# Turning the second head pair's q and k on TensorE in the prologue, another bank for the first row maximum, and two weight forms three products later

## The chip, the cores and the metric

The kernel runs on one core of one Trainium2 chip. The metric is the time of one execution of the program on the device in microseconds. The engines are TensorE (PE; its weight loads are PEld), VectorE (DVE), ScalarE (ACT), GpSimd (POOL) and SyncE (SP); SP, ACT and POOL also issue DMA transfers.

## The reference

Routed attention over 4 batches, 8 heads, 768 tokens and head size 64, and behind it a feed-forward block over 3072 tokens, 512 model columns and 2048 hidden columns. All inputs are float32.

```
q_n, k_n, c_n = q, k, centroids, each row divided by its norm
q_assign = argmax over the 16 clusters of q_n . c_n        (k_assign likewise)
scores = (q @ k.T) / 8, and -1e9 where q_assign != k_assign
attn   = softmax(scores) along the keys
x      = attn @ v, heads side by side            # 3072 x 512
h      = x @ w_in                                # 512 x 2048
g      = h * erf(softplus(h))
out    = g @ w_out                               # 2048 x 512
```

## The kernel before

**Attention.** Heads go in pairs: 16 pairs of one batch and two heads, each pair with the two heads' 64 dimensions side by side on the 128 partitions. For pair `p` the kernel needs q and k turned, with dimensions on partitions and 768 tokens along the row (`rows[p % 3]`, called `qT` and `kT`). The normal way there: `load` brings q (or k) in pieces of 32 tokens by 32 dimensions, four loads a tensor, 128 bytes at a time, in such an order that one VectorE instruction over 128x768, which turns each 32x32 block (`ve.transpose` in `transposes`), gives `qT`. For pair 1 the load goes into `x_more`, a tile that later holds other things: right behind the turn of pair 1's k, `fetch(PLACES - 1)` loads a block of `w_in` into it. v is loaded with tokens on partitions, two loads a pair, 256 bytes at a time.

A pair then goes through these steps. `similarities` multiplies by the centroids, `choose` finds each token's cluster on VectorE, and `masks` writes cluster rows `qm` and `km` (ScalarE or VectorE copies them from PSUM). `vectors` makes bf16 copies `qv` and `kv`. `maxima_step(p, i, sm)` makes, for one of six tiles of 128 queries and one half of the keys, masked scores in the PSUM tile `sm` by a pass of `kv` with `qv` and a pass of `km` with `qm`, and one VectorE reduction over 128x768 takes the row maximum (`nmx`) from it. Steps 0 to 5 are the first half of a pair's queries, 6 to 11 the second. After steps 5 and 11 a short reduction writes `lowest`; `turn` moves these values with six matmuls into a row of the bank `turned` and ScalarE copies them into the first rows of `qm`. From there on, `period(p, i)` is the steady state: `products` and `scores` (TensorE), `curve` (exponentials on ScalarE), `accumulate` (sums on GpSimd), `attend` (product with v), with the next maxima between them (`step_ahead`).

**PSUM.** There are two whole banks `turned[0]` and `turned[1]`, the tile `wide` of two banks, which takes the maxima in the steady state, and two tiles of two banks for scores (pool `ps_s`). In the prologue the first of these is taken under the name `also` and alternates with `wide` for pair 0's first six maxima.

**The prologue** is the last part of the function ahead of `for p in range(NPAIR)`. It prepares pair 0 and turns pair 1's q (between the mask copies and the first maximum) and k (behind the first `turn`). `warm(n, bank, rhs)` issues `n` matmuls whose result nobody reads. The calls through `te`, `ve`, `ae`, `ge` and `sy` are kept in the order in which they are written, so each engine's order in the prologue is that of the code.

**The feed-forward block** replaces blocks of matrix products by sums and differences of blocks ("forms") and fewer products. `project26(n)` is the second product of chunk `n`: 26 products numbered 0 to 25 (`RIGHT` names the right operand, `LEFT` the left one), each of four accumulating steps, which the profile shows as eight matmuls. Left operands that are sums are made on VectorE by `LEFT_STEPS`, whose first entry is the product behind which they stand. Right operands numbered from 100 are loaded from DRAM (`b_dram`) through a ring of three places on SP's queue (`load_stream`, issued behind every product that uses such an operand, for the one three further on). The right operands' own forms are made once, on the way: most on GpSimd, but the two of `SLOW_FORMS` on VectorE within `project26(0)`, in two pieces each. The first makes slot 5, which product 19 uses; the second, made from it, is stored in `b_dram` and is what product 25 loads. `last_forms[p]` holds the pieces that stand behind product `p`, ahead of that product's left steps on VectorE. Behind them comes `evict`, which takes the results out of PSUM one product late.

In the profile nearly every instruction carries line 137, the helper that records it, so groups are told apart by the tiles' names. The slow forms show as `more_out<-w_out,more_out` and `x_own<-more_out,w_out`, the left steps as `g<-g` or `g_more<-g`.

Of the kernel before, what the change touches and what calls it, by code (L numbers as in the profile page):

```python
# [19 lines left out]
P = 128  # L20
B, H, S, D = 4, 8, 768, 64
C = 16
NJ = S // P
Q = 32
# [42 lines left out]
SLOW_FORMS = [(5, -7, 0, -1, None), (11, 5, -1, 1, 9)]  # L67
# [78 lines left out]
def kernel(  # L146
# [13 lines left out]
    te, ve, ae, ge = (  # L160
        InOrder(tc, e, in_order) for e in (nc.tensor, nc.vector, nc.scalar, nc.gpsimd)
    )
# [8 lines left out]
    turned = [ps.tile([P, 512], F32, name=f"turned{i}") for i in range(2)]  # L171
# [12 lines left out]
    def passing(name, bufs, **kw):  # L184
        return attention.enter_context(tc.tile_pool(name=name, bufs=bufs, **kw))

    ps_s = passing("ps_s", 2, space=PSUM)
    wide = passing("ps_w", 1, space=PSUM).tile([P, 2, 512], F32, name="wide")
# [7 lines left out]
    ident = const.tile([P, P], F32, name="ident")  # L196
# [10 lines left out]
    lows = [  # L207
        {nm: const.tile([P, S], BF16, name=f"{nm}{i}") for nm in ("qv", "kv", "qm", "km")}
        for i in range(2)
    ]  # L210
# [4 lines left out]
    rows = [{nm: const.tile([P, S], F32, name=f"{nm}T{i}") for nm in "qk"} for i in range(2)]  # L215
# [5 lines left out]
    pairs = {}  # L221
    sy = InOrder(tc, nc.sync, in_order)
    queues = [sy, ae]

    def heads(p):
        return p // HP, 2 * (p % HP)

    def load(p, nm, src, pl):
        if p >= NPAIR:
            return  # L230
        b, h0 = heads(p)
        if nm == "v":
            t = pl.tile([P, NJ, 2, D], F32, name="in_v")
            for e in range(2):
                queues[0].dma_start(out=t[:, :, e], in_=src[b, h0 + e].rearrange("(j p) d -> p j d", p=P))
        else:

            if pl is None:
                t = x_more.rearrange("p a k t -> p (a k t)")[:, (nm == "k") * S : (1 + (nm == "k")) * S]
                t = t.rearrange("p (n t) -> p n t", t=Q)  # L240
            else:
                t = pl.tile([P, NB, Q], F32, name="in_" + nm)
            for e in range(2):
                for g in range(D // Q):
                    queues[e if nm == "q" else e * g].dma_start(
                        out=t[e * D + g * Q : e * D + (g + 1) * Q],
                        in_=src[b, h0 + e, :, g * Q : (g + 1) * Q].rearrange("(n t) d -> t n d", t=Q),
                    )
        pairs.setdefault(p, {})[nm] = t

    def load_qk(p):
        load(p, "q", q, stage if p != 1 else None)
        load(p, "k", k, stage if p != 1 else None)
# [18 lines left out]
    for base, pattern, sign, op, fill in (  # L272
# [5 lines left out]
            out=first, in_=first, compare_op=op, fill=fill, base=base, pattern=pattern,  # L278
# [115 lines left out]
    def transposes(p, which="qk"):  # L394

        if p >= NPAIR:
            return
        st = pairs[p]
        for nm in which:
            st[nm + "T"] = rows[p % 3][nm]  # L400
            ve.transpose(out=st[nm + "T"], in_=st.pop(nm).rearrange("p n t -> p (n t)"))
        if "k" in which:
            st.update(lows[p % 2])
            if p > 1:
                load_qk(p + 1)
# [14 lines left out]
    def choose(p, spare=None, aside=False):  # L420

        if p >= NPAIR:
            return
        st = pairs[p]
        n = HW // C
        sims = routep.tile([P, HW], F32, name="sims")
        ve.transpose(out=sims, in_=st.pop("psim"))
        yield
        sim = sims.rearrange("p (g c) -> p g c", c=C)
        mx = (wide[:, 0] if spare is None else spare)[:, 512 - n :]  # L430
        ve.reduce_max(out=mx, in_=sim, axis=AX.X)
        yield
        hot = routep.tile([P, HW], BF16, name="hot")
        ve.tensor_tensor(
            out=hot.rearrange("p (g c) -> p g c", c=C), in0=sim,
            in1=mx.unsqueeze(2).to_broadcast([P, n, C]), op=ALU.is_equal,
        )
        yield
        if aside:
            st["aside"] = routep.tile([P, HW], BF16, name="aside")  # L440
            ve.transpose(out=st["aside"][D + Q :], in_=hot[D : D + Q])
            yield
        st["hotT"] = routep.tile([P, HW], BF16, name="hotT")
        ve.transpose(out=st["hotT"], in_=hot)
# [31 lines left out]
    def maxima_step(p, i, sm=wide, behind=False, cut=HW):  # L476

        st = pairs[p]
        nmx = maxima[p % 2]
        t, half = divmod(i, 2)  # L480
        keys = slice(cut, S) if half else slice(0, cut)
        width = keys.stop - keys.start

        def passes(a, b, start, rows):
            for e in range(2):
                r = slice(e * D + rows.start, e * D + rows.stop)
                te.matmul(
                    sm[:, e, 0:width], lhsT=st[a][r, t * P : (t + 1) * P],
                    rhs=st[b][r, keys], start=start, stop=not start,
                )  # L490

        passes("qv", "kv", True, slice(0, D))
        if behind:
            yield
        passes("qm", "km", False, slice(Q, D) if behind else slice(0, D))
        if behind:
            yield
        ve.tensor_reduce(
            out=nmx[:, :, t, half], in_=sm[:, :, 0:width], axis=AX.X, op=ALU.max, negate=True
        )  # L500
        if i in (NJ - 1, 2 * NJ - 1):
            h = i // NJ
            ve.tensor_reduce(
                out=lowest[h][:, :, ::D].rearrange("p t e -> p e t"),
                in_=nmx[:, :, h * HJ : (h + 1) * HJ], axis=AX.X, op=ALU.min,
            )
            turns.append((p, h))
# [21 lines left out]
    def products(u):  # L529
        p, half, j = units[u]  # L530
        if u in sc_of:
            return
        st = pairs[p]
        sc = sc_of[u] = ps_s.tile([P, 2, 512], F32, name="sc", tag="s")
        for e in range(2):
            r = slice(e * D, (e + 1) * D)
            te.matmul(
                sc[:, e, 0:HW], lhsT=st["kT"][r, j * P : (j + 1) * P],
                rhs=st["qT"][r, half * HW : (half + 1) * HW], start=True, stop=False,
            )  # L540
# [280 lines left out]
    def forms26(steps, engine=ge):  # L821
        work = []
        for f in (0, 2):
            for o, a, b, sign, k in steps:

                def piece(f=f, o=o, a=a, b=b, form=plus_of if sign > 0 else minus_of, k=k):
                    form(place26(o, f), place26(a, f), place26(b, f), engine)
                    if k is not None:
                        stored = b_dram[k].rearrange("p (f m) -> p f m", f=FG)
                        sy.dma_start(out=stored[:, f : f + 2], in_=place26(o, f))  # L830

                work.append(piece)
        return work
# [385 lines left out]
    def project26(n, plan=None):  # L1219
# [22 lines left out]
        q = OUT_ORDER.index(n)  # L1242
# [42 lines left out]

        last_forms = {p: sum((forms26([step]) for step in LAST_FORMS[p]), []) if not n else [] for p in LAST_FORMS}
        if not n:
            for step, p in zip(SLOW_FORMS, (9, 11)):
                for i, piece in enumerate(forms26([step], ve)):
                    last_forms[p + i] = [piece]  # L1290
        run(f() for f in curves.get(-1, []) + gates_at.get(-1, []) + last_forms[-1])
# [50 lines left out]
    def run(work):  # L1342
        for _ in work:
            pass
# [125 lines left out]
    def warm(n, bank, rhs):  # L1470
        for _ in range(n):
            te.matmul(bank[:, 0 : rhs.shape[-1]], lhsT=identb, rhs=rhs, start=True, stop=True)

    zeros = lowest[1].rearrange("p t n -> p (t n)")
# [7 lines left out]
    for e in range(2):  # L1482
        ae.copy(
            out=ccT[e * D : (e + 1) * D, :, e * C : (e + 1) * C],
            in_=pct[e * D : (e + 1) * D].rearrange("d (r e c) -> d r e c", e=2, c=C)[:, :, e],
# [7 lines left out]
    for r in (0, D):  # L1493
        for half in range(2):
            for e in range(2):
                c = r + half * Q + e * C
                ve.tensor_copy(
                    out=pick[r : r + D, half, e * D : (e + 1) * D].rearrange("p (n c) -> p n c", n=2)[:, :, 1 : C + 1],
                    in_=first[r : r + D, c : c + C].unsqueeze(1).to_broadcast([D, 2, C]),
                )  # L1500
    also = ps_s.tile([P, 2, 512], F32, name="sc", tag="s")
    products(0)
    warm(9, turned[0], zeros)
    run(choose(0))
    copies = [
        masks(0, nm, half, bank)
# [2 lines left out]
    ve.tensor_scalar_max(out=st["qm"][:, 0:HW], in0=wide[:, 0, 0:HW], scalar1=0.0)  # L1509
    for copy in copies[1:]:  # L1510
        copy()
    transposes(1, "q")
    load(0, "v", v, vp)
    for n in range(PLACES - 1):
        fetch(n)
    for i in range(NJ):
        run(maxima_step(0, i, also if i % 2 else wide))
        if i == 1:
            masks(0, "q", 1, turned[1])()
        if i < NJ - 1:  # L1520
            warm(2, turned[0], zeros)
    step_ahead(0)
    warm(2, turned[0], zeros)
    turn(0, 0)
    turns.clear()
    transposes(1, "k")
    fetch(PLACES - 1)
    queues[0] = queues[1] = nc.sync
    for p in range(NPAIR):
# [55 lines left out]
    )  # L1585
    hidden(0, 1, {0: store(4)}, first=ve.tensor_copy)
    project26(0)
    hidden26(1, {0: adds, 2: lambda: load_x(2, sy)})
    copy49(3, 6)
# [37 lines left out]
```

## Time and profile before

| | us |
|---|---|
| median of 3 runs | 949.17 (949.16 to 949.69) |
| the profiled execution | 949.11 |
| its span, first to last instruction | 947.3 |
| TensorE busy | 938.7 |
| VectorE busy | 754.2 |
| ScalarE busy | 560.7 |
| GpSimd busy | 523.9 |

Times in the profile count from the start of the span. In a line of the timeline the first number is the start, the second the time from the first start to the last end of the instructions that the line merges (`x8` is eight), and the bracket at the end is how long the engine had stood idle and what ended that. Busy times of TensorE hold modelled ends, so starts are the better evidence. In the chain of work that ended last, a line is a start, a length and the group that held the chain.

### The profile page before, as it was taken

What the parts mean: (1) busy time and instruction counts of PE and PEld (TensorE: products, weight loads), DVE (VectorE), ACT (ScalarE), POOL (GpSimd) and SP (SyncE); (2) the same over time, 40 slices, a digit from 0 to 9 for tenths busy, and PEclk for the clock granted to TensorE, in tenths of its full rate; (3) what the DMA queues carried; (4) which work ended last, traced back from release to release, by engine and by line L of the source; (5) the groups of instructions that cost most, each with busy time, mean ns of one, the idle gap of its engine ahead of it and who ended that gap; (6) DMA issues with size and microseconds to landing.
All of it is one profiled execution on the core that took longest, in us unless ns stands there. A gap on an engine that the chain in (4) does not pass through costs nothing.

```text
span 947.3 us, 20932 instructions
## 1 busy us (share of the span) xinstructions
PE 938.7 (99%) x8151; PEld 692.0 (73%) x8151; DVE 754.2 (80%) x1336; ACT 560.7 (59%) x880; POOL 523.9 (55%) x353
## 2 busy tenths in 40 slices
PE   8999999999999999999999999999999999999998
PEld 3555555555555555588888888888888888888887
DVE  8888888888888888788995778456796974768977
ACT  3788888888888877576423541357825225574341
POOL 1688888888888888999605010676600028770000
PEclk9999999999999999999999999999999999999999
DMA  9444444444444521664659987545645535523443
GB/s 216 85 114 112 111 108 109 113 113 113 111 113 97 123 58 35 224 225 186 222 188 229 204 197 249 166 145 178 199 139 174 158 109 156 178 90 121 149 131 111
DMA packets 183360, 138.74 MB, mean 146 GB/s; under 512 B 132032, under 2 KB 141248, under 8 KB 183232
## 3 DMA queue, kind: packets, MB, share of 16 engines
q1 hardware_dynamic: 176048, 127.83, 46.7%
q0 software_dynamic: 4720, 9.18, 5.5%
q8 instruction: 64, 1.05, 0.4%
q10 hardware_dynamic: 2496, 0.43, 0.2%
q14 instruction: 32, 0.26, 0.1%
HBM read 99.39 MB, written 39.85 MB: 147 GB/s over the span
## 4 chain that ended last, share of the span: by engine, by line
PE 49%; DVE 1%; issue 0%
PE bank L137 40%; PE turned L137 9%; DVE g L137 1%; DVE g_more L137 0%; DVE osb L137 0%; DVE more_out L137 0%; DVE x_own L137 0%
## 5 line engine op out<-in xcount | busy, mean ns | idle before, releaser
L137 POOL TENSOR_TENSOR more_out<-more_out,pr 128x768 f32<-128x768 f32 x128 | 223.8, 1749 | 14.3 <-ACT pr L137 5.7
L137 DVE TENSOR_REDUCE nmx<-wide 128x2 f32<-128x512 f32 (+2 forms) x189 | 180.5, 955 | 51.7 <-PE wide L137 51.1
L137 ACT ACTIVATE pr<-sc 128x768 f32<-128x768 f32 x192 | 148.6, 810 | 65.2 <-PE wide L137 59.2
L137 PE MATMUL turned<-pr,in_v 128*32 128x193 f32 x3072 | 144.8, 330 | 0.0
L137 PEld LDWEIGHTS turned<-pr,in_v 128*32 128x32 f32 x3072 | 91.5, 109 | 51.5 <-issue 26.2
L137 PE MATMUL sc<-qT,kT 64*128 64x384 f32 x528 | 98.8, 488 | 0.0
L137 POOL TENSOR_TENSOR more_out<-pr,pr 128x768 f32<-128x768 f32 x32 | 60.8, 1899 | 41.7 <-ACT pr L137 41.7
L137 POOL TENSOR_TENSOR u<-w_in 128x1 f32<-128x1 f32 x2 | 0.4, 190 | 139.2 <-DVE w_in L137 139.2
L137 DVE TENSOR_TENSOR g<-g 128x512 f32<-128x512 f32 x88 | 61.9, 703 | 16.2 <-PE bank L137 8.8
L137 PE MATMUL bank<-g_more,g 128*128 128x256 f32 x296 | 70.0, 379 | 0.0
L137 PE MATMUL bank<-x_own,more_in 128*128 128x256 f32 x276 | 68.1, 379 | 0.0
L137 PE MATMUL bank<-g_more,more_in 128*128 128x256 f32 x288 | 66.4, 380 | 0.0
L137 PE MATMUL wide<-kv,qv 64*128 64x256 bf16 (+2 forms) x378 | 64.0, 328 | 1.4 <-DVE nmx L137 0.9
L137 PE MATMUL wide<-km,qm 64*128 64x256 bf16 (+3 forms) x378 | 62.6, 327 | 0.0
L137 PEld LDWEIGHTS sc<-qT,kT 64*128 64x128 f32 x528 | 47.3, 187 | 20.6 <-ACT inv L137 3.4
L137 ACT ACTIVATE x_own<-x_own 128x512 int32<-128x512 uint32 (+3 forms) x62 | 62.1, 1014 | 0.0
L137 PEld LDWEIGHTS bank<-g_more,g 128*128 128x128 f32 x296 | 56.2, 190 | 7.9 <-issue 0.3
L137 PEld LDWEIGHTS bank<-g_more,more_in 128*128 128x128 f32 x288 | 54.6, 190 | 8.2 <-DVE g L137 0.8
L137 PEld LDWEIGHTS bank<-x_own,more_in 128*128 128x128 f32 x276 | 52.4, 190 | 7.1
L137 DVE TENSOR_TENSOR g<-g,bank 128x256 f32<-128x256 f32 (+1 forms) x83 | 41.1, 513 | 20.4 <-PE bank L137 13.6
L137 ACT ACT_TABLE_LOAD x36 | 46.2, 1283 | 16.5 <-DVE g L137 15.9
L137 PEld LDWEIGHTS <-qv 64*128 64x128 bf16 x384 | 23.2, 93 | 42.8 <-issue 26.6
(251 smaller groups left out, 2072.2 us busy)
## 6 DMA issues: line engine op xcount, KB each, us to landing
g_more<-b_dram SPq DMA_DIRECT2D x57, 512.0 KB, 3.6
more_in<-a_dram SPq DMA_DIRECT2D x98, 256.0 KB, 2.6
x_own<-in_moe_w_in_dram SPq DMA_DIRECT2D x13, 512.0 KB, 4.0
in_v<-in_v_dram SPq DMA_DIRECT2D x32, 192.0 KB, 3.0
x_dram<-more_out SPq DMA_DIRECT2D x128, 48.0 KB, 2.3
x_own<-x_dram SPq DMA_DIRECT2D x6, 1024.0 KB, 6.7
a_dram<-w_in SPq DMA_DIRECT2D x12, 512.0 KB, 3.8
in_k<-in_k_dram SPq DMA_DIRECT2D x59, 96.0 KB, 2.6
```

Of the source, the lines that this page charges most:

```text
L137: ins = getattr(self.engine, name)(*args, **kw)
```

## The change

- Pair 1's q and k are loaded with tokens on partitions, as v is: two loads a tensor in place of four, 256 bytes at a time.
- They are turned on TensorE, six tiles of 128x128 float32 for each tensor, into the banks `turned[0]` and `turned[1]`, and ScalarE copies them from there to `rows[1]`. The first three tiles of q stand where four of nine warm-ups stood (the other five now write `also`); the other nine tiles stand behind maxima steps 0 to 4, in place of two warm-ups each. The two VectorE instructions that turned pair 1's q and k go.
- The six first maxima begin in `also` in place of `wide`. Step 5 so falls to `wide`, which step 6 (`step_ahead(0)`) uses as before.
- The four pieces of `SLOW_FORMS` stand behind products 12, 13, 14 and 15 of `project26(0)` in place of 9, 10, 11 and 12.

```
             if pl is None:
                 t = x_more.rearrange("p a k t -> p (a k t)")[:, (nm == "k") * S : (1 + (nm == "k")) * S]
-                t = t.rearrange("p (n t) -> p n t", t=Q)
+                t = t.rearrange("p (j e d) -> p j e d", e=2, d=D)
+                for e in range(2):
+                    queues[0].dma_start(out=t[:, :, e], in_=src[b, h0 + e].rearrange("(j p) d -> p j d", p=P))
             else:
                 t = pl.tile([P, NB, Q], F32, name="in_" + nm)
-            for e in range(2):
+            for e in range(2 * (pl is not None)):
...
-            for step, p in zip(SLOW_FORMS, (9, 11)):
+            for step, p in zip(SLOW_FORMS, (12, 14)):
...
     products(0)
-    warm(9, turned[0], zeros)
+    by_tokens = {nm: pairs[1].pop(nm) for nm in "qk"}
+    for nm in "qk":
+        pairs[1][nm + "T"] = rows[1][nm]
+    pairs[1].update(lows[1])
+
+    def turned_tiles(nm, tiles, bank):
+        for j, tile_of in enumerate(tiles):
+            te.transpose(
+                out=bank[:, j * P : (j + 1) * P], in_=by_tokens[nm][:, tile_of].rearrange("p e d -> p (e d)"),
+                identity=ident,
+            )
+        ae.copy(
+            out=rows[1][nm][:, tiles[0] * P : (tiles[-1] + 1) * P], in_=bank[:, 0 : len(tiles) * P]
+        )
+
+    turned_tiles("q", (0, 1, 2), turned[0])
+    warm(5, also[:, 0], zeros)
     run(choose(0))
...
-    transposes(1, "q")
     load(0, "v", v, vp)
...
     for i in range(NJ):
-        run(maxima_step(0, i, also if i % 2 else wide))
+        run(maxima_step(0, i, wide if i % 2 else also))
         if i == 1:
             masks(0, "q", 1, turned[1])()
         if i < NJ - 1:
-            warm(2, turned[0], zeros)
+            turned_tiles(*(("q", (3, 4)), ("q", (5,)), ("k", (0, 1)), ("k", (2, 3)), ("k", (4, 5)))[i], turned[i == 3])
     step_ahead(0)
     warm(2, turned[0], zeros)
     turn(0, 0)
     turns.clear()
-    transposes(1, "k")
     fetch(PLACES - 1)
```

## The prediction

> **What bounds the kernel now.** I read the page's head and its busy line first, then the busy times by stage, then the chain of work that ended last, and only then the timeline around the two places that the change touches.
>
> ```profile
> span 947.3 us, 20932 instructions
> PE 938.7 (99%) x8151; PEld 692.0 (73%) x8151; DVE 754.2 (80%) x1336; ACT 560.7 (59%) x880; POOL 523.9 (55%) x353
> ```
>
> ```profile
> 10.00:26.00 16.00, 14.38 (x131) 5.76 (x131) 14.49 (x21) 6.96 (x11) 2.67 (x2) 1.00 1.01 269
> 26.00:375.00 349.00, 348.88 (x5055) 194.87 (x5052) 299.00 (x478) 282.22 (x457) 288.37 (x171) 1.00 0.44 101
> ```
>
> The first row is the page's span, the second its busy time by engine. In the stage rows the columns are the stretch, its length, then PE, PEld, DVE, ACT, POOL busy time. From 26 to 375 us TensorE is busy 348.88 of 349.00 us: there is no slack in which a later or earlier start could be lost, so what the prologue gains or loses up to 26 us is worth the same at the end. Only before that (14.38 of 16.00) does TensorE wait. The chain that ended last names the second place:
>
> ```profile
> 473.26 0.60 DVE more_out L137
> ...
> 475.14 0.60 DVE more_out L137
> ...
> 476.68 0.60 DVE x_own L137
> ...
> 479.48 23.55 PE bank L137 x108
> ```
>
> Up to 479.48 us the chain runs on VectorE; from there it is TensorE nearly to the end. Three of VectorE's pieces in it, 0.60 us each, are the last out-weight forms, which the change moves.
>
> **Part 1, the last out-weight forms three products later.** The timeline there:
>
> ```profile
> 475.32 1.89 PE L137 MATMUL bank<-more_out,g 128*128 128x256 f32 x8
> ...
> 477.05 1.89 PE L137 MATMUL bank<-g_more,g 128*128 128x256 f32 x8
> 477.19 2.14 DVE L137 TENSOR_TENSOR g<-g 128x512 f32<-128x512 f32 x3
> 477.30 4.11 SPq L137 DMA_DIRECT2D b_dram<-x_own  x2
> ...
> 479.48 3.69 PE L137 MATMUL bank<-w_out,g 128*128 128x256 f32 x16 [0.53 <-DVE g L137]
> ...
> 494.30 1.41 DVE L137 TENSOR_TENSOR g<-g 128x512 f32<-128x512 f32 x2
> ...
> 494.88 3.43 PEld L137 LDWEIGHTS bank<-w_out,g 128*128 128x128 f32 x16
> ```
>
> A product of project26(0) is eight matmuls and takes 477.05 - 475.32 = 1.73 us (0.216 a matmul). Product 14 was due at 477.05 + 1.73 = 478.78 and began at 479.48: a stall of 0.70 us, for its left operand, made by the last of the three steps at 477.19, which end at 479.33. Three of the four moved pieces stand on VectorE ahead of these steps (products 9, 10, 11), 3 x 0.60 = 1.80 us. Without them the steps end at 477.53, over a microsecond before 478.78, and the whole 0.70 us goes.
>
> What is late next: the four pieces now stand at products 12 to 15. Behind product 15 VectorE has done the same work as before, so it stands where it stood in absolute time, with TensorE 0.70 us earlier. The narrowest place that I find is product 24: the last left step ends at 494.30 + 1.41 = 495.71; its weight load, eight after 494.88, falls at 494.88 + 1.73 = 496.61, with the change at 495.91. It holds by 0.20 us. The two stores of the second form (at 477.30) go behind one more operand load on SP's queue, and the load at product 16 then waits behind them for VectorE's last piece at product 15; that operand is used six products, 6 x 1.73 = 10.4 us, later, so even a wait of some microseconds is covered. I cost this at nothing; if the cover at product 24 failed it would cost a few tenths, at worst the 0.70 again. Part 1: **-0.70 us**, bounds -0.70 and 0.
>
> **Part 2, the prologue.** Rows of the timeline:
>
> ```profile
> 4.29 2.54 SPq L137 DMA_DIRECT2D x_more<-in_q_dram  x4
> ...
> 5.38 0.45 PE L137 MATMUL turned<-ident,pr 128*128 128x128 f32 x1
> ...
> 9.16 1.64 PE L137 MATMUL turned<-lowest,identb 128*128 128x384 bf16 x9
> ...
> 10.86 0.32 PE L137 MATMUL wide<-hotT,pick 64*128 64x384 bf16 x1
> ...
> 11.22 0.56 DVE L137 TENSOR_SCALAR qm<-wide 128x384 bf16<-128x384 f32 x1 [0.41 <-PE turned L137]
> 11.25 1.05 ACT L137 ACTIVATE km<-turned,nbig 128x384 bf16<-128x384 f32 x2 [2.90 <-PE turned L137]
> 11.69 0.97 DVE L137 STREAM_TRANSPOSE qT<-x_more 128x768 f32<-128x768 f32 x1
> ...
> 12.08 0.34 PE L137 MATMUL wide<-km,qm 64*128 64x384 bf16 x2
> ...
> 12.36 0.50 PE L137 MATMUL turned<-lowest,identb 128*128 128x384 bf16 x2
> 12.59 0.92 DVE L137 TENSOR_REDUCE nmx<-wide 128x2 f32<-128x768 f32 x1
> 12.79 0.34 PE L137 MATMUL sc<-kv,qv 64*128 64x384 bf16 x2
> ...
> 13.94 1.42 SPq L137 DMA_DIRECT2D in_v<-in_v_dram  x2
> ...
> 16.95 0.95 DVE L137 TENSOR_REDUCE nmx<-sc 128x2 f32<-128x768 f32 x1
> 17.09 0.34 PE L137 MATMUL wide<-kv,qv 64*128 64x384 bf16 x2 [0.20 <-DVE nmx L137]
> ...
> 17.52 0.50 PE L137 MATMUL turned<-lowest,identb 128*128 128x384 bf16 x2
> 18.02 0.18 DVE L137 TENSOR_REDUCE lowest<-nmx 128x6 bf16<-128x18 f32 x1
> ...
> 18.25 0.34 PE L137 MATMUL turned<-identb,lowest 128*32 128x128 bf16 x6 [0.23 <-DVE lowest L137]
> ...
> 18.97 0.97 DVE L137 STREAM_TRANSPOSE kT<-x_more 128x768 f32<-128x768 f32 x1
> ...
> 20.50 0.96 DVE L137 TENSOR_REDUCE nmx<-wide 128x2 f32<-128x768 f32 x1 [0.56 <-PE wide L137]
> ...
> 21.51 0.34 PE L137 MATMUL wide<-kv,qv 64*128 64x384 bf16 x2 [0.27 <-DVE nmx L137]
> ```
>
> The prologue's end hangs on the turn at 18.25: the first maxima go through it into the mask rows, and everything on TensorE stands behind it in order. So I ask when the turn comes.
>
> *The k transpose* (18.97, 0.97 us) goes. VectorE waited 0.56 us for TensorE right behind it (20.50), so this is worth nothing.
>
> *The q transpose* (11.69, 0.97 us) goes, and the first maxima go to the other bank, whose first pass need not wait for the mask copies. The second pass needs qm, done at 11.22 + 0.56 = 11.78, and the first km, about then; it can go at about 11.92, where before the first pass went, instead of 12.08. Its maximum then starts near 12.30 in place of 12.59: -0.29.
>
> *The transposes on TensorE.* Six maxima start from 12.59 to 16.95, 0.87 us apart, and TensorE's steps are as long, so a longer step shows at once. Two warm-ups with their switch took 12.79 - 12.36 = 0.43. Two float32 transposes take 2 x 0.216 = 0.43 at the spacing of full-array float32 matmuls in part 1; from above, the one transpose of the trace (5.38) lasted 0.45, two 0.90. I take 0.50, nearest to the rows of many matmuls, since the single one stands alone at the start: +0.07 at each of four steps of two tiles, +0.28, which takes the 0.29 back. The step of one tile also has a mask product and waits for ScalarE's copy of the bank, and comes out even. Bounds for the sixth maximum: -0.29 and 4 x 0.47 - 0.29 = +1.59; taken 0.
>
> A rule of the Trainium skill (VectorE: DVE Perf Modes, "The three transpose paths") gives 390 ns for a 128x128 bf16 transpose on TensorE in isolation, and would price two at 0.78; by it the sum below would be 1.1 us higher, inside the bounds. No run yet shows transposes in a row.
>
> *The last two maxima in one bank.* Steps 0 to 5 now alternate from `also`, so step 5 ends in `wide`, and step 6 (17.09) writes `wide` too. Before, it had only to wait for the fourth maximum. Now it waits for the sixth to end, 0.95 us after its start, and 0.05 more (20.50 + 0.96 to 21.51). Behind it in TensorE's order stand two warm-ups, then the turn: 17.52 - 17.09 = 0.43 to the warm-ups and 0.43 through them. The turn comes 0.95 + 0.05 + 0.86 = 1.86 after the sixth maximum starts; before, 18.25 - 16.95 = 1.30 (it waited for `lowest`, 18.02). **+0.56 us**, and the work behind moves with it, since TensorE waits for VectorE at 21.51 and VectorE for TensorE at 20.50 in turn.
>
> *Loads.* Landing rows for the two shapes:
>
> ```profile
> in_v<-in_v_dram SPq DMA_DIRECT2D x4, 192.0 KB, 4.9
> ...
> x_more<-in_q_dram SPq DMA_DIRECT2D x4, 96.0 KB, 2.8
> ```
>
> Pair 1's q is now two loads in v's shape, 0.71 us of SP each (13.94) where four took 2.54. The second is issued near 5.0 and lands between 7.8 (2.8) and 9.9 (4.9); the transposes want it at 9.16, where warm-ups stood. I take the early side, because v's loads shared the queue with the weights. Three transposes and five warm-ups take 0.65 + 5 x 0.18, no more than nine took (1.64), so the masks at 10.86 hold. The copies, five of two tiles or fewer and one of three, go on ScalarE:
>
> ```profile
> 457.87 0.35 ACT L137 COPY g_more<-bank 128x256 f32<-128x256 f32 x1
> ```
>
> 0.35 us each, under the masks' work on an engine that idled 2.90 us before 11.25. Free.
>
> **The sum.** 0 + 0.56 - 0.70 = -0.14 us on the profiled execution (949.11 us, its span and 1.81 around it), which lies 0.06 under the median, 949.17. Bounds: -0.29 + 0.56 - 0.70 = -0.43, and +1.59 + 0.56 - 0.70 = +1.45. Forecast **949.0 us**.
>
> **Rivals.**
> 1. The transposes fit the steps and the earlier start is kept: 949.17 - 0.43 = 948.7. For it: 0.43 against 0.43. Against: float32 weights load longer and the bank waits for a copy. It could go a little lower if the next stages pack better.
> 2. Another wait takes the stall at product 14 (the 0.20 us at product 24, or a store ahead of an operand load): part 1 gives nothing, 949.17 + 0.56 = 949.7.
> 3. Pair 1's q lands at 9.9: the masks are late by 0.75, so 949.0 + 0.75 = 949.8.
> 4. The other side: TensorE loses its rate. At the start it runs slower:
>
> ```profile
> 2.41 2.95 PE L137 MATMUL turned<-pick,identb 128*128 128x256 bf16 x13 [2.41 <-DVE fixed L137]
> ```
>
> That is 2.95 / (13 x 256) = 0.89 ns a column, against 1.64 / (9 x 384) = 0.47 at 9.16. The slow stretch lasted at least from 2.41 to 5.36 and ended before 9.16. If ten transposes in place of ten warm-ups leave too little ordinary matmul between 12 and 17 us, and the rate falls for some 4.5 us (between 2.95 and 6.75), that costs half of it, 2.2 us: 951.2. It decides if it falls at all; one short stretch is enough. Against it: some 0.33 us of matmuls remain in each 0.87, and the 0.56 us wait before 11.92 brought no slow rate. The Trainium skill (TensorE: Matmul & The Clock Gate, "Part 4: PE-mode transpose") says that a transpose does not count as busy for the clock gate, which speaks against this change; the granted clock in the view reads 1.00 even in the slow first stretch, so no trace here shows it.
>
> **How the numbers follow.** Forecast 0.56, rival 1 0.16, rival 2 0.10, rival 3 0.08, rival 4 0.10. 0.2% is 1.9 us, about what a measurement of this kernel can tell from no change. Only rival 4 is past it: slower 0.10. Faster would need four times the gain of rival 1's end; I give it 0.02 of rival 1's 0.16. Same 0.88. The range runs from just under rival 1, 948.4, to the upper bound of the transposes, 949.17 + 1.45 = 950.6; outside it are rival 4 and rival 1's tail.
>
> **What would show it.** Right: no wait on VectorE ahead of product 14, products 1.73 us apart through product 25, the forms at products 12 to 15; step 6 waiting for the sixth maximum in `wide`, and the turn near 18.8. Wrong: the turn before 18.4 (rival 1) or past 19.5 (transposes far apart), a new wait between products 15 and 25, masks later than 10.9, or bf16 matmuls near 0.9 ns a column after 9 us.

## The result and the profile after

The changed kernel takes **950.82 us** (median of 17 runs, 950.71 to 951.24; the kernel before in the same comparison 949.17). The ratio is 1.0018, with a 95% interval of 1.0010 to 1.0025: slower by 1.65 us, which is small but clear of the noise, where 949.0 was forecast. The profiled execution took 950.83 us, 1.72 more than that of before (949.11). Where these 1.72 us come from can be read from the starts of TensorE's matmuls, the same matmul in both traces:

```
stretch (us of before)                       shift of TensorE, after - before
to the turn of the first maxima (18.25)      +0.22
at 127                                       -0.28
at 180 to 184                                +0.87 and +0.10
at 253 to 257                                +0.87 and +0.10
product 14 of project26(0), 479.5            -0.70
from there to the end of the span            -0.12
span, after - before                         +1.06
outside the span (1.84 -> 2.50)              +0.66
```

Two of these terms are the prologue and the forms that the change set out to move. The others lie where nothing was edited. The start of the prologue itself shifts from one execution to the next (the first mask product, 10.86 in the prediction's rows, starts between 10.80 and 11.31 in the traces). From that product to the turn it takes 7.39 us in the kernel before and in every run below with its prologue, and 7.59 to 7.60 in the changed kernel and every run with its unaltered prologue, so the +0.22 is the prologue's own. First the parts that were edited. The page's head and the busy times by stage, columns as in the prediction:

```profile
span 948.3 us, 20921 instructions
```

```profile
10.00:26.00 16.00, 13.47 (x127) 5.91 (x126) 12.66 (x19) 8.82 (x17) 2.45 (x2) 1.00 0.93 252
26.00:375.00 349.00, 347.62 (x5017) 193.64 (x5020) 299.73 (x475) 280.52 (x455) 286.82 (x171) 1.00 0.43 101
```

From 26 to 375 us TensorE was busy 348.88 us before and is busy 347.62 now: idle time has appeared in the stretch in which there was none. The timeline of the prologue:

```profile
12.16 0.44 PE L137 MATMUL turned<-ident,x_more 128*128 128x128 f32 x2
...
12.27 0.96 DVE L137 TENSOR_REDUCE nmx<-sc 128x2 f32<-128x768 f32 x1 [0.48 <-PE sc L137]
...
12.71 0.33 PE L137 MATMUL wide<-km,qm 64*128 64x384 bf16 x2
...
16.60 0.95 DVE L137 TENSOR_REDUCE nmx<-wide 128x2 f32<-128x768 f32 x1
...
17.61 0.34 PE L137 MATMUL wide<-kv,qv 64*128 64x384 bf16 x2 [1.21 <-DVE nmx L137]
...
18.47 0.34 PE L137 MATMUL turned<-identb,lowest 128*32 128x128 bf16 x6
```

Two transposes take 0.44 us, the maxima stand as close as before ((16.60 - 12.27) / 5 = 0.87), the sixth starts 0.35 earlier than before (16.95), step 6 waits 1.21 us for it in its own bank, and the turn comes 0.22 later than before (18.25). Around product 14:

```profile
477.24 1.89 PE L137 MATMUL bank<-more_out,g 128*128 128x256 f32 x8
...
477.44 2.14 DVE L137 TENSOR_TENSOR g<-g 128x512 f32<-128x512 f32 x3
...
478.97 1.89 PE L137 MATMUL bank<-g_more,g 128*128 128x256 f32 x8
```

Product 14 starts at 478.97, 1.73 behind product 13, with no wait: the stall of 0.70 is gone.

**Where nothing was edited.** Of the waits of TensorE (in total, times, longest) one stands in the answer of after alone:

```profile
PE turned L137 <- DVE sims L137: 1.4, 2, 0.7
```

One of the two is at 180.98 us. The timeline there, after:

```profile
175.24 0.19 DVE L137 TENSOR_REDUCE lowest<-nmx 128x6 bf16<-128x18 f32 x1
...
175.77 0.98 DVE L137 STREAM_TRANSPOSE more_out<-in_k 128x768 f32<-128x768 f32 x1 [0.35 <-DMA x_dram<-more_out]
...
177.25 1.96 DVE L137 TENSOR_TENSOR w_in<-w_in,fixed 128x512 f32<-128x512 f32 x1
...
179.13 1.21 DVE L137 TENSOR_REDUCE nmx<-wide 128x2 f32<-128x1024 f32 x1
...
180.26 0.57 DVE L137 STREAM_TRANSPOSE sims<-turned 128x384 f32<-128x384 f32 x1
...
180.98 0.53 PE L137 MATMUL turned<-more_out,fixed 128*32 128x192 f32 x8 [0.69 <-DVE sims L137]
```

and before:

```profile
175.48 0.98 DVE L137 STREAM_TRANSPOSE more_out<-in_k 128x768 f32<-128x768 f32 x1
...
176.98 0.68 DVE L137 TENSOR_TENSOR w_in<-w_in,fixed 128x512 f32<-128x512 f32 x1
...
178.22 1.23 DVE L137 TENSOR_REDUCE nmx<-wide 128x2 f32<-128x1024 f32 x1 [0.56 <-PE wide L137]
...
179.36 0.57 DVE L137 STREAM_TRANSPOSE sims<-turned 128x384 f32<-128x384 f32 x1
...
180.17 0.51 PE L137 MATMUL turned<-more_out,fixed 128*32 128x192 f32 x8
```

The k transpose of a later pair starts 0.35 us after VectorE became free. Two instructions on, the maximum that bounds a block of decoded weights (`bounded_apart` in `period(p, 3)`; its second input is a constant in `fixed`) lasts 1.96 us in place of 0.68. The transpose of the similarities comes 0.90 later, and TensorE, which needs the same bank next, waits 0.69. What GpSimd does then, after and before:

```profile
176.98 1.68 POOL L137 TENSOR_TENSOR more_out<-more_out,pr 128x768 f32<-128x768 f32 x1
```

```profile
177.05 2.16 POOL L137 TENSOR_TENSOR more_out<-more_out,pr 128x768 f32<-128x768 f32 x1
```

Before, VectorE's maximum began 0.07 us ahead of GpSimd's addition (176.98, 177.05), kept its 0.68, and the addition took 2.16. After, the addition is 0.27 ahead (176.98, 177.25), keeps its 1.68, and the maximum ends 0.55 behind it (179.21, 178.66). At both places the one that started first kept its time and the other took longer. The Trainium skill (SBUF — State Buffer, "Who interferes with whom") says that a VectorE instruction with two inputs from SBUF contends with a GpSimd instruction that reads SBUF, since the second input comes through a read interface that the two share, and that the order of issue decides who is blocked. This trace agrees, with 1.96 against 0.68 on the one side and 2.16 against 1.68 on the other. The groups of this maximum (minimum, median and longest in ns) show that it happened twice, in the periods of pairs 6 and 9. After, then before:

```profile
L137 DVE TENSOR_TENSOR w_in<-w_in,fixed x8: 681/681/1957, 55.7 to 226.5; 128x512 f32<-128x512 f32 x8
L137 DVE TENSOR_TENSOR w_out<-w_out,fixed x6: 681/682/1948, 251.2 to 373.4; 128x512 f32<-128x512 f32 x6
```

```profile
L137 DVE TENSOR_TENSOR w_in<-w_in,fixed x8: 681/681/682, 55.4 to 225.6; 128x512 f32<-128x512 f32 x8
L137 DVE TENSOR_TENSOR w_out<-w_out,fixed x6: 681/681/682, 249.9 to 371.5; 128x512 f32<-128x512 f32 x6
```

What remains is why the transpose starts late. The profile names a store of x_dram, which is only the last event that it saw. **Theory A**: an engine pauses for 0.3 to 0.4 us at fixed places of its own instruction list, and the change moved these places. Counted in the trace from 0, semaphore waits included, VectorE's entry 319 is the late transpose in the period of pair 6 and entry 447 the last wait ahead of the one in the period of pair 9. In the kernel before these transposes are entries 325 and 454, six later, since two transposes and four waits stood ahead of them in the prologue. **Theory B**: the transposes do wait for that store, through the four loads fewer on SP's queue.

### The profile page after: what moved, and what is told of

Its sections match the earlier page's. It is cut to its first block, busy times and chain, and to the rows that moved or that the text cites. A ratio compares the mean times of both kernels' runs of the same rounds, so it can differ in the third digit from the quotient of the medians.

```text
span 948.3 us, 20921 instructions
## 1 busy us (share of the span) xinstructions
PE 938.2 (99%) x8149; PEld 692.5 (73%) x8149; DVE 755.0 (80%) x1334; ACT 562.8 (59%) x886; POOL 522.9 (55%) x353
## 4 chain that ended last, share of the span: by engine, by line
PE 94%; DVE 3%; ACT 1%; POOL 1%; DMA 1%; issue 1%; SPq 0%; DVEq 0%; POOLq 0%
PE bank L137 47%; PE turned L137 26%; PE sc L137 16%; PE wide L137 5%; DVE nmx L137 1%; DMA x_dram<-more_out 1%; POOL more_out L137 0%; ACT pr L137 0%; DVE sims L137 0%; DVE more_out L137 0%; ACT x_own L137 0%; ACT qm L137 0%; DVE w_out L137 0%; DVE w_in L137 0%; ACT inv L137 0%
```

## The experiments

**e1_forms_alone**: the kernel before with the third part of the change only.

```
-            for step, p in zip(SLOW_FORMS, (9, 11)):
+            for step, p in zip(SLOW_FORMS, (12, 14)):
```

> Only the last out-weight forms are moved (products 12 and 14), the prologue is as before. All theories agree here: the stall of 0.70 us at product 14 goes and nothing else changes, 949.17 - 0.70 = 948.5 us. If the forms themselves were to blame for the loss, it would be 949.2 or above.

Measured 948.72 us (948.43 to 948.75; before on that chip 949.34), ratio 0.9992 (0.9983 to 1.0000). Product 14 starts 1.72 us behind product 13 (479.14 and 477.42 in its timeline): the stall of 0.70 is gone, and TensorE shows no other step of more than 0.1 us against the kernel before. The part is worth what its stall was.

**e2_pad6** and **e3_pad3**: the changed kernel with six or three one-column fills on VectorE behind the first turn, which bring its list up to, or halfway up to, its old length.

```
     turns.clear()
+    for _ in range(6):                      # range(3) in e3_pad3
+        ve.memset(fixed[:, Q + 2 : Q + 3], 0.0)
```

> The changed kernel with six VectorE memsets of one column behind the first turn, where VectorE idles 1.6 us. Theory A: VectorE pauses some 0.35 us at fixed places of its own instruction list (63 past a multiple of 128 entries); the change took six entries out ahead of the steady state, and so moved a pause onto the k transposes near 175 and 249 us; the maximum with w_in (w_out) behind it then comes after GpSimd's addition instead of ahead of it and takes 1.96 us, not 0.68, and TensorE stalls 0.87 + 0.10 us each time. Six entries more put the pauses back: both maxima take 0.68 us, and the time is 950.82 - 1.94 = 948.9 us. Theory B: the transposes wait there for a store of x (the releaser that the waits name), which depends on the order of the loads; the memsets change nothing, 950.8 us.

> The same with three memsets. Theory A with its count: the pause falls three entries earlier, on the short reduction that writes lowest, right ahead of the transpose, which is then late just the same: both long maxima stay, 950.8 us. If any idle padding helps (theory A without its count) 948.9 us. Theory B: 950.8 us.

e2_pad6 took 948.87 us (948.60 to 949.28), ratio 0.9996 (0.9987 to 1.0005), 1.95 less than the changed kernel for six instructions more. The k transposes start without a pause, and the long maxima are gone (the one of 835 ns, at 201 us, has its like in the changed kernel, 0.82 us at 202, and delays TensorE in neither):

```profile
L137 DVE TENSOR_TENSOR w_in<-w_in,fixed x8: 681/681/835, 55.8 to 225.7; 128x512 f32<-128x512 f32 x8
L137 DVE TENSOR_TENSOR w_out<-w_out,fixed x6: 681/681/682, 250.0 to 371.6; 128x512 f32<-128x512 f32 x6
```

Theory B is refuted: loads and stores are those of the changed kernel. e3_pad3 took 949.02 (948.87 to 949.58), ratio 0.9996 (0.9988 to 1.0005), also without long maxima, where my count had them stay. Entry 319 is there the short reduction `lowest` right ahead, whose predecessor keeps VectorE busy for 0.96 us. So a pause can hide behind a running instruction; e11_pad1 below tests the rule that this suggests.

**e4_before_less6**: the kernel before with setup fills moved from VectorE to GpSimd; VectorE's list is five entries shorter.

```
-    ve.memset(ccT, 0.0)
+    ge.memset(ccT, 0.0)
...
-        ve.memset(t, FLOOR)
+        ge.memset(t, FLOOR)
...
-    ve.memset(minus, -1.0)
-    ve.memset(alleps, S * EPS)
-    ve.memset(two, 2.0)
+    ge.memset(minus, -1.0)
+    ge.memset(alleps, S * EPS)
+    ge.memset(two, 2.0)
```

> The kernel before, with six memsets of the setup moved from VectorE to GpSimd: VectorE's list is six entries shorter ahead of the steady state, as in the change, and nothing else of the change is there. Theory A: the two long maxima (1.96 us) appear near 175 and 249 us, 949.17 + 1.94 = 951.1 us. Theory B: 949.2 us.

949.61 us (949.49 to 952.85; before 949.34), ratio 1.0005 (0.9997 to 1.0014): one long maximum in place of two.

```profile
L137 DVE TENSOR_TENSOR w_in<-w_in,fixed x8: 681/681/1954, 55.4 to 226.3; 128x512 f32<-128x512 f32 x8
L137 DVE TENSOR_TENSOR w_out<-w_out,fixed x6: 681/681/681, 250.6 to 372.2; 128x512 f32<-128x512 f32 x6
```

With nothing of the change in it, a shorter list makes the same collision at the same place. At pair 9 entry 447 is the first of the two waits ahead of the transpose, and no pause shows. The time rose by less than the 0.97 of one collision, and is not clear of the noise: TensorE is 0.96 later behind that place, but 0.28 earlier at 127 us, since ScalarE's list is one entry longer here and its pause (e10_scalar4 below) moved as well.

**e5_prologue_alone**: the changed kernel with `SLOW_FORMS` at 9 and 11 again.

> The change without its third part: the last out-weight forms stand at products 9 and 11 again. The forms work on VectorE after 450 us, so its list up to 375 us is that of the changed kernel. Theory A (pauses at fixed entries of VectorE's list, each turned into about 0.97 us by the port that VectorE and GpSimd share): both long maxima of 1.95 us stay, the stall of 0.70 us ahead of product 14 is back, and the time is 950.82 + 0.70 = 951.5 us. Theory B (a store in the way of the k transposes): the same. If the two parts of the change worked on each other, the time would lie elsewhere, down to 950.8.

951.83 us (951.48 to 952.18; before 949.23), ratio 1.0027 (1.0016 to 1.0038). Both collisions are there and the stall is back: product 14 starts 2.41 us behind product 13 (481.45 and 479.04 in its timeline) where 1.73 is due. Nothing in TensorE's starts shows the two parts of the change working on each other. It is 0.3 above the forecast, which lies at the lower edge of what its executions show.

**e7_delay**: the kernel before, with VectorE held up ahead of the k transpose in two periods.

```
         elif i == 2:
+            if p in (6, 9):
+                ve.reduce_max(out=fixed[:, Q + 2 : Q + 3], in_=two.to_broadcast([P, 300]), axis=AX.X)
             transposes(p + 2, "k")
```

> The kernel before the change, with one VectorE reduction over 300 columns (some 0.37 us) put ahead of the k transpose in pairs 6 and 9 and nothing else. Theory A: the delay lets GpSimd's addition go ahead of VectorE's two-input maximum, which then lasts 1.95 us in place of 0.68 at both places; TensorE is 0.87 to 0.97 us later at each, and the time is 949.3 + 1.9 = 951.2 us. Rival: VectorE has 0.56 us to spare behind the maximum (its next one waits that long for TensorE), so a delay of 0.37 us is absorbed and the time stays 949.3; the loss of the changed kernel then has another cause than the delay.

951.07 us (950.87 to 951.43; before 949.23), ratio 1.0020 (1.0011 to 1.0029). Groups, then the timeline at pair 6:

```profile
L137 DVE TENSOR_TENSOR w_in<-w_in,fixed x8: 681/681/2041, 55.9 to 227.0; 128x512 f32<-128x512 f32 x8
L137 DVE TENSOR_TENSOR w_out<-w_out,fixed x6: 681/681/2080, 251.6 to 373.9; 128x512 f32<-128x512 f32 x6
L137 DVE TENSOR_REDUCE fixed<-fixed x2: 455/456/456, 175.8 to 249.7; 128x1 f32<-128x300 f32 x2
```

```profile
175.82 0.46 DVE L137 TENSOR_REDUCE fixed<-fixed 128x1 f32<-128x300 f32 x1
176.19 0.97 DVE L137 STREAM_TRANSPOSE more_out<-in_k 128x768 f32<-128x768 f32 x1
...
177.66 2.04 DVE L137 TENSOR_TENSOR w_in<-w_in,fixed 128x512 f32<-128x512 f32 x1
```

This execution runs 0.43 later than that of before from the turn on; beyond this the maximum at 177.66 comes 0.25 late (before: 176.98), where that of the changed kernel comes 0.33 late (177.25 in an execution that runs 0.06 earlier there). A delay of this size alone makes the loss: TensorE is 1.0 us later behind each of the two places. The 0.56 us that VectorE has to spare there do not absorb it.

**e8_one_input**: the changed kernel, with the maximum's second input taken away.

```
     def bounded_apart(n):
         w = w_steps[n][0]
-        ve.tensor_tensor(out=w, in0=w, in1=two.to_broadcast([P, LC]), op=ALU.max)
+        ve.reduce_max(out=w, in_=w.unsqueeze(2), axis=AX.X)
```

> The changed kernel with the two-input maximum that bounds the weights replaced by a reduction of the same 512 columns onto themselves, which has one input; the lower bound of 2.0 on the decoded weights is left out. The list of VectorE keeps its length, so the k transposes of pairs 6 and 9 still start 0.35 us late. Theory A: without a second input from SBUF there is nothing to wait for; the operation takes 0.55 to 0.7 us at all places, TensorE loses nothing at 180 and 253 us, and the time is 950.82 - 1.94 = 948.9 us. Rival: the late transpose itself costs the time, through the similarities behind it: 950.8 us, or in between.

948.94 us (948.66 to 949.09; before 949.23), ratio 0.9997 (0.9988 to 1.0006):

```profile
176.09 0.98 DVE L137 STREAM_TRANSPOSE more_out<-in_k 128x768 f32<-128x768 f32 x1 [0.35 <-DMA x_dram<-more_out]
...
177.57 0.67 DVE L137 TENSOR_REDUCE w_in<-w_in 128x512 f32<-128x512 f32 x1
178.47 1.23 DVE L137 TENSOR_REDUCE nmx<-wide 128x2 f32<-128x1024 f32 x1 [0.24 <-PE wide L137]
```

The transpose is as late as in the changed kernel, by 0.35, and costs nothing: VectorE still has 0.24 to spare. GpSimd's addition is not lengthened either: behind a maximum that starts just ahead of it it takes 1.68 to 1.69 in this run, against 2.12 to 2.16 in the kernel before. So the pause takes 0.35 us and the shared port makes 0.97 of it. e7 and e8 together show both links.

**e11_pad1**: one fill, as in e2_pad6 with `range(1)`.

> The changed kernel with one one-column fill on VectorE after the prologue. Theory A with the rule read from the runs so far: the pause comes at every 64th odd place of the list (entries 319 and 447 among them) and shows only where the entry before it has not kept the engine busy, that is on a k transpose or on the second of the two waits ahead of it, and is hidden on the first wait and earlier. With one entry more, entry 319 is the second wait of pair 6, and 447 the first wait of pair 9: one long maximum (pair 6, 1.95 us), none at pair 9, and about 950.82 - 0.97 = 949.85 us. The rival that any shift of the list takes both away gives 948.9; that the number of entries does not matter, 950.8.

949.88 us (949.51 to 950.66; before 949.23), ratio 1.0007 (0.9998 to 1.0016), with one long maximum, at pair 6:

```profile
L137 DVE TENSOR_TENSOR w_in<-w_in,fixed x8: 681/682/1957, 56.0 to 226.9; 128x512 f32<-128x512 f32 x8
L137 DVE TENSOR_TENSOR w_out<-w_out,fixed x6: 681/681/682, 251.2 to 372.8; 128x512 f32<-128x512 f32 x6
```

The entries of all kernels, counted in the traces (pair 6 has entry 319, pair 9 entry 447):

```
kernel            k transpose  entry 319 / 447 is          late starts   time
before            325, 454     far ahead / far ahead       none          949.2
e2_pad6           325, 454     far ahead / far ahead       none          948.87
e3_pad3           322, 451     lowest / maximum ahead      none          949.02
e4_before_less6   320, 449     second wait / first wait    0.35, none    949.61
e11_pad1          320, 449     second wait / first wait    0.35, none    949.88
after             319, 448     transpose / second wait     0.35, 0.37    950.82
```

**e10_scalar4**: the kernel before, with four one-column copies on ScalarE.

```
     warm(9, turned[0], zeros)
+    for i in range(4):
+        ae.copy(out=fixed[:, Q + 4 + i : Q + 5 + i], in_=two)
     run(choose(0))
```

> The kernel before, with four copies of one column on ScalarE in the prologue, where it waits for TensorE: ScalarE's list is as long as in the changed kernel, and nothing else is changed. Theory A (pauses at fixed entries of each engine's list): the late start of a curve at 125.8 us (0.28 us, ScalarE) is gone, with nothing changed on VectorE, so TensorE is 0.28 us earlier from 127 us on: 949.23 - 0.28 = 948.95 us. If the time outside the span hangs on ScalarE's list, it rises here from 1.8 to about 2.4 and the total is 949.6 us; if on SP's, it stays.

948.80 us (948.66 to 949.22; before 949.23), ratio 0.9995 (0.9986 to 1.0004). A curve on ScalarE, in the kernel before (entry 191 of ScalarE's list) and here (entry 195):

```profile
125.82 0.81 ACT L137 ACTIVATE pr<-sc 128x768 f32<-128x768 f32 x1 [1.18 <-PE turned L137]
```

```profile
125.78 0.81 ACT L137 ACTIVATE pr<-sc 128x768 f32<-128x768 f32 x1 [0.90 <-PE wide L137]
```

It waits 1.18 us and 0.90: the 0.28 that the changed kernel gains at 127 us is the same pause, taken off ScalarE's curve by four entries more. The total alone is not clear of the noise; the starts of TensorE are: they step by -0.26 at 127 us. The time outside the span did not move (1.80).

**e6_pads_banks**, **e9_sync4**, **e12_tensor4**: the changed kernel with six fills in an idle place of VectorE and the first maximum in `wide` again; then, on top, four one-element loads on SP's queue; then two short warm-ups as well.

```
     for copy in copies[1:]:
         copy()
+    for _ in range(6):
+        ve.memset(fixed[:, Q + 2 : Q + 3], 0.0)
...
-        run(maxima_step(0, i, wide if i % 2 else also))
+        run(maxima_step(0, i, also if i % 2 else wide))
...
     fetch(PLACES - 1)
+    for i in range(4):                                          # e9_sync4, e12_tensor4
+        sy.dma_start(out=fixed[0:1, Q + 4 + i : Q + 5 + i], in_=centroids[0, 0:1, i : i + 1])
...
     warm(5, also[:, 0], zeros)
+    warm(2, also[:, 0], identb)                                 # e12_tensor4
```

> The changed kernel with VectorE's list brought back to its old length by six one-column fills, put where VectorE waits for TensorE before the first maximum, and with the first maximum in the old bank again (wide, also, ...), so that step 6 no longer waits for the sixth maximum in its own bank. Theory A: no long maximum between 40 and 375 us; the sixth maximum starts near 16.6, the turn 1.30 behind it at 17.9 (18.25 before the change); TensorE ends 0.35 (start) + 0.28 (ScalarE's late curve at 125.8, gone) + 0.70 (product 14) = 1.33 us earlier than before the change, so 948.0 us, or 948.5 if the half microsecond outside the span that the new prologue showed stays. The rival, that the shared bank costs nothing because the next wait takes its place: 948.9, as with the fills alone.

> The version with six fills and the old bank order (948.21 us), with four loads of one element each added to SP's queue after the prologue, so that SP's list has again the 845 entries that it has in the kernel before. This looks for the time outside the span: 1.8 us in the kernel before and in the kernels with its prologue, 2.3 to 2.5 in all with the new one, whatever VectorE's list. If it hangs on the length of SP's list, the time outside falls back to about 1.8 and the total to 947.7 us; if it hangs on ScalarE's list or on TensorE's, both stay: 2.3 outside, 948.2 us.

> The version with six fills, the old bank order and four small loads (947.96 us, 2.2 us of it outside the span), with two short warm-up matmuls more behind the five in the prologue, where TensorE waits for VectorE: its matmuls and weight loads are then as many as in the kernel before. If the time outside the span hangs on the length of TensorE's list, it falls from 2.2 to 1.8 and the total to 947.6 us; if not, both stay (948.0). The span itself should stay at 945.8.

e6_pads_banks took 948.21 us (948.04 to 948.51; before 949.23), ratio 0.9990 (0.9981 to 0.9998). Step 6 and the turn:

```profile
16.73 0.94 DVE L137 TENSOR_REDUCE nmx<-sc 128x2 f32<-128x768 f32 x1
...
16.87 0.34 PE L137 MATMUL wide<-kv,qv 64*128 64x384 bf16 x2 [0.34 <-DVE nmx L137]
...
18.03 0.34 PE L137 MATMUL turned<-identb,lowest 128*32 128x128 bf16 x6 [0.23 <-DVE lowest L137]
```

The wait of 1.21 us is 0.34, and the turn comes 1.30 behind the sixth maximum, as in the kernel before. From the first mask product to the turn it takes 7.13 us, 0.26 less than there. e9_sync4 took 947.96 (947.68 to 948.31), ratio 0.9987 (0.9978 to 0.9996), and e12_tensor4 948.03 (947.60 to 948.22; before 949.09), ratio 0.9988 (0.9979 to 0.9997). These three beat both kernels; between the last two nothing can be told. The time outside the span is 2.31, 2.18 and 2.18 in them, 2.51 in the changed kernel, 1.80 in before. The lengths of SP's, ScalarE's and TensorE's lists have each been put back or tried, and most of the difference stayed; putting SP's back took off 0.13, neither the 0.5 nor the nothing that e9_sync4 expected. It differs with VectorE's list too: 2.48 to 2.51 in the three kernels where it is shortest, 2.29 with one fill, 2.43 with three, 2.30 with six. What makes it is open; e5_prologue_alone (2.48) and e1_forms_alone (1.87) place it in the new prologue.

## Why the prediction was wrong, point by point

- **Part 1, -0.70: right**, in the changed kernel and alone. No other wait took its place up to product 25, nor did a store (rival 2).
- **The earlier start, -0.29: right** (-0.35 at the sixth maximum). **The transposes' +0.28: wrong.** I took 0.50 for two where 0.44 was measured (and not 0.78, the other price that the prediction names), so they fit the steps and the earlier start was kept, as rival 1 had it. The row of 0.216 for a full-array float32 matmul priced them well; the single transpose of 0.45 did not.
- **Two maxima in one bank: right.** 1.86 from the sixth maximum to the turn was forecast and 1.87 measured. Undone, with the fills moved to an idle place, it gave 0.66 (948.87 to 948.21, on two chips; 0.55 when each is set against its own before, 0.47 from the first mask product to the turn). With the term before, the prologue cost +0.22 where +0.56 was forecast.
- **q lands in time** (transposes at 9.17, masks at 10.87) **and TensorE keeps its rate** (two bf16 passes 0.33 to 0.34 as before): rivals 3 and 4 did not come.
- **The step that failed** is the one by which everything from 26 to 375 us was a plain shift: no slack, so nothing lost or gained there, and two VectorE instructions fewer worth nothing once their own place was covered. The stretch has no slack for TensorE, but its rhythm hangs on an order of arrival between VectorE and GpSimd with a margin of 0.06 to 0.10 us, fourteen times. Two pauses of 0.35 us turned it round, each for 0.97, and a third, on ScalarE, went: +1.94 - 0.28. By my own terms as measured, without these, the sum would be 0.22 - 0.70 = -0.48, that is 948.7; e2_pad6 (948.87) and e8_one_input (948.94), which keep the change and lose the collisions, came within 0.3 of it, though they also hold the 0.28 and the rise outside the span. I had costed the removed instructions by their duration and not asked what their removal shifts.
- **The time outside the span** was held constant at 1.81, without a reason given. It rose by 0.66, and this part of the loss is not explained.

## What to carry to other kernels

Where a tuned loop repeats, look for two engines that start an instruction on the same port within a tenth of a microsecond of each other, and ask what a third of a microsecond on either of them would do: that margin, not the busy share, says how robust the loop is. An edit that only takes instructions off an engine's list moves all that follows on that list, so a change of a few tenths should be tried with a few idle instructions put back before it is judged. A group whose longest duration differs from its median (681/681/1957) points to such a collision at a glance.

## What the hardware did that I had not expected

VectorE and ScalarE paused 0.28 to 0.37 us at places 128 entries apart in their lists (entry 63 and every 128th behind it), where the entry ahead did not keep them busy for as long. The two that decided this case are VectorE's 319 and 447; at others the pause was hidden, where `lowest` or a maximum stood at the place or VectorE waited anyway. All fourteen traces bear it out on ScalarE: where it had idled for at least 0.3 us when a wait ended, the instruction behind the wait started 0.32 us after it in all 16 cases at such places (entries 191, 447 and 575), and within 0.25, mostly 0.04, in all of some 1600 others.

That the pause is the fetch of the next block of instructions is an inference and not shown. For it speak the packets of the instruction queue in the page of after:

```profile
q14 instruction: 32, 0.26, 0.1%
```

0.26 MB in 32 packets is 8 KB each. The lists of VectorE, ScalarE, GpSimd and SyncE have 1720, 1192, 580 and 841 entries in this trace, which is 13 + 9 + 4 + 6 = 32 full blocks of 128. The trace also has the time of each packet: behind the late starts on VectorE (175.77 and 249.63) one begins at 176.70 and 250.32, and in the kernel before, behind ScalarE's late curve (125.82), one at 126.85. The Trainium skill (Runtime: NRT & Kernel Launch, "Instruction fetch mechanics") has the list refilled in blocks of 256 instructions, at a cost that is mostly hidden; here the distance is 128 entries, and at two places the pause was not hidden and led to the loss of 0.97 each.

The other surprise is the leverage of the shared port: one instruction of 0.68 us, started 0.27 behind GpSimd's, lasted 1.96, and TensorE lost 0.97.
